# Attention and a gated unit on one core: six of nine blocks of gates and values in Strassen's seven products, with the weight sums made on chip

## The chip, the cores and the metric

The kernel runs on one core of a Trainium2 chip. The time is the device time of one execution in microseconds, from several executions on the same chip. The profile is that of one execution and names the core's engines: PE (TensorE, the matmuls; PEld is its weight load), DVE (VectorE), ACT (ScalarE), POOL (GpSimd) and SP, which here only issues DMAs. All arithmetic is on float32 data.

## The reference

`q`, `k`, `v` are (8, 8, 576, 64): eight batches of eight heads. Four heads see a local window of 32 positions, four see every 32nd position. The result, 4608 tokens by 512, goes through a gated unit with 1536 hidden columns.

```python
scores = scale * np.matmul(q, k.transpose(0, 1, 3, 2))
scores = np.where(masks[None], scores, -1000000000.0)
attn = np.exp(scores - np.max(scores, axis=-1, keepdims=True))
attn = attn / (np.sum(attn, axis=-1, keepdims=True) + 1e-09)
x = np.matmul(attn, v)                       # then reordered to (4608, 512)
gate = 1.0 / (1.0 + np.exp(-(x @ w_gate)))   # w_gate, w_val: 512 x 1536
val = x @ w_val
return (gate * val @ w_out)                  # w_out: 1536 x 512
```

## The kernel before

**Blocks and columns.** The tokens are cut into nine blocks `k` of 512 (`TB`). Blocks 0 to 7 are the first 512 positions of each batch; block 8 (`B`) gathers the 64 remaining positions of all eight (kept in `xr` by `keep_rest`, L328, until then). The hidden columns are cut into twelve groups `f` of 128 (`NF`). One (k, f) has three steps of twelve matmuls each: `glu_gate` (L385) makes the gate in PSUM bank "g" and ACT takes its sigmoid into tile `e`; `glu_val` (L393) makes the value in bank "v", DVE multiplies the two (L407); `glu_out` (L444) multiplies the result with `w_out` and adds it up over f in four banks "o0", "o1".

**Three matmuls for one product.** A factor is kept as a rounded upper part in the type float32r and the rest: `xh`, `xl` for the input, `wh`, `wl` for weights, `hh`, `hl` for the hidden block. `products` (L378) multiplies upper by upper, upper by rest and rest by upper, for each of four chunks of 128 input rows: twelve matmuls of 128 x 128 weights on 512 columns. The upper part is an ACT cast (L402), the rest a DVE subtraction (L405).

**Attention.** A pair of heads (`pair`, L163) is one step; a batch has four, each giving one chunk of 128 rows of x. A step is: load q and k (Q), scores on PE (S), mask, maximum and subtraction on DVE (F, L224 to L230), exponential on ACT (E, L234), sum, reciprocal and multiplication on DVE (N, L238 to L241), eight transposes of 32-row strips on DVE (B, L263), then the values on PE (X, L291), and from PSUM the two parts of x (H, L322, and L, L326). The pairs of batches 0 and 1 and the block 0 of the gated unit stand in an order written out by hand (`ORDER`). The 24 pairs of batches 2 to 7 are issued by `attention()` between the blocks: pair n's values and pair n + 1's scores after the gate and value of every third f of blocks 1 to 6, while `glu_out` runs one or two f behind. Scores there take banks "g" and "v", values bank "a".

**Order.** From block 1 on PE runs its instructions in the order of the program. The other engines' order is fixed by a scheduler that goes through the program in order and, where an instruction isn't ready by its own model of time, takes the next that is. Each engine then keeps that order on the chip: an instruction that waits holds all behind it. SP issues the loads and the outputs in one queue.

Of the kernel before, what the change touches and what calls it, by code (L numbers as in the profile page):

```python
# [9 lines left out]
F32 = mybir.dt.float32  # L10
# [10 lines left out]
P = 128  # L21
# [25 lines left out]
LATE = NF - 1  # L47

# [34 lines left out]
def attention_then_glu(ctx, tc, qk_l, qk_s, v_l, v_s, w_all, consts, out):  # L83
# [79 lines left out]
    def pair(b, step, space):  # L163
# [111 lines left out]
        def weigh(xp):  # L275
# [4 lines left out]
            for n in range(NBL if local else NG):  # L280
# [3 lines left out]
                for j in range(2):  # L284
# [14 lines left out]
            if local:  # L299
                full = ns // 2 * P  # L300
                src = xp.rearrange("p (r n) -> p r n", r=2)[:, :, :full].rearrange("p r (u n) -> p u r n", n=per * LB)
                main = [(src, lambda x: x[:, c, :].rearrange("p (u r n) -> p u r n", r=2, n=per * LB))]
                left = [(xp[:, full : full + REST], lambda x: x)]
            else:
# [3 lines left out]
                runs = [(0, 2 * (SS // 2), GC, 0), (BANK, full, GC, half), (BANK + full * GS, 1, STRIDE - half - full * GC, half + full * GC)]  # L308
                for at, n, r, first in runs:
                    src = xp[:, at : at + n * GS].rearrange("p (g i r) -> p i g r", i=CLS, r=GC)[:, :, :, :r]  # L310
# [16 lines left out]

        def keep_rest():  # L328
# [6 lines left out]
            L=split_low, R=keep_rest,  # L335
        )

# [3 lines left out]
    def attention():  # L341

        todo = [(b, step) for b in range(BY_PE, B) for step in range(4)]
        ahead, now = pair(*todo[0], work), None
        ahead["Q"]()
        for n, (b, step) in enumerate(todo + [(B, 0)]):
            if now:
                of, p = todo[n - 1]
                if p == 0:
                    x_tiles(of)  # L350
                    left_over(of)
                now["X"](bank("a", f"x{of}_{p}"))
                now["H"](), now["L"](), now["R"]()
            if b < B:
                now = ahead
                now["Z"]()
                if n == 0:
                    now["S"](bank("a", f"s{b}_{step}"))
                else:
                    now["S"](*(ps.tile([P, BANK], F32, tag=t, name=f"s{b}_{step}_{t}") for t in "gv"))  # L360
                now["F"](), now["V"](), now["E"](), now["N"](), now["B"]()
                if n + 1 < len(todo):
                    ahead = pair(*todo[n + 1], work)
                    ahead["Q"]()
            yield

    def split_rest():
        x_tiles(B)
        xh, xl = xs[B]
        for c in range(NC):  # L370
            for b, x in xr.items():
                cut = slice(b * REST, b * REST + x.shape[2])
                nc.scalar.copy(xh[:, c, cut], x[:, c, :])
                nc.vector.tensor_tensor(xl[:, c, cut], x[:, c, :], xh[:, c, cut].bitcast(F32), op=ALU.subtract)
# [17 lines left out]

    def glu_val(k, f, v=None):  # L393
# [3 lines left out]
        e, t = hs[k, f], work.tile([P, TB], F32, tag="t", name=f"t{k}_{f}")  # L397
        hh = work.tile([P, TB], F32R, tag="hh", name=f"hh{k}_{f}", bufs=3)
        hl = work.tile([P, TB], F32R, tag="hl", name=f"hl{k}_{f}", bufs=3)
        hs[k, f] = (hh, hl)  # L400
# [43 lines left out]
    def glu_out(k, *fs):  # L444

        if fs[0] == 0:
            two = [bank(f"o{n}", f"o{k}_{n}") for n in range(NTT // 2)]
# [73 lines left out]
    with tc.manual_schedule(engines={mybir.EngineType.PE}):  # L521
        last = [(0, NF - 1)]
        pend = attention()
        for k in range(1, NB):
            if k == B:
                split_rest()
# [97 lines left out]
```

## Time and profile before

| | us |
|---|---|
| median of 3 runs | 993.3 (992.32 to 997.05) |
| the profiled execution | 991.66 |
| its span, first to last instruction | 989.8 |

The mean granted clock of TensorE was 0.987 of full speed. A page of the profile gives each engine's busy time and its share of the span, then the chain of work that ended last, followed backwards, then groups of instructions: line, engine, operation, output and inputs, shape, count, busy time in us, mean duration in ns, and idle time of the engine before them with what ended it. Views of the trace give single instructions in order of time (start and duration in us), busy time by stretches, and waits (in total, times, longest). The whole-page rows that are used stand with the argument below.

### The profile page before, as it was taken

The page shows a single profiled execution, that of the slowest core. Times are in us where ns is not written, and L with a number is a line of the kernel's source. Part 1 is how long each engine was busy: PE and PEld are TensorE (multiplying, and loading weights), DVE is VectorE, ACT ScalarE, POOL GpSimd, SP SyncE. Part 2 cuts the span into 40 slices and gives each one's busy share as a digit, 9 for nine tenths or more (in the row PEclk, how much of TensorE's full clock was granted, in tenths as well). Part 3 has the DMA queues.
Part 4 walks back from the last instruction along what each step waited for, and adds up shares of the span by engine and source line. Part 5 has one row for each costly group of instructions (what it writes and reads, how often), then busy time and mean ns, then how long its engine had stood idle before and what let it go on. Part 6 is the DMA issues. An engine that isn't in the chain of part 4 may idle for free.

```text
span 989.8 us, 17820 instructions
## 1 busy us (share of the span) xinstructions
PE 968.3 (98%) x7840; PEld 797.7 (81%) x7840; DVE 492.4 (50%) x861; ACT 335.9 (34%) x587; POOL 3.5 (0%) x20
## 2 busy tenths in 40 slices
PE   4999999999999999999999999999999999999998
PEld 4787778888888888888888888888888888888886
DVE  6788875555555555454544555555545421112111
ACT  4787863232323233322322333223223311112111
POOL 0000000000000000000000000000000000000000
PEclk7799999999999999999999999999999999999999
DMA  7666632111211112111201121112110010001001
GB/s 262 198 185 221 220 114 68 41 53 42 95 41 53 42 63 73 53 42 51 66 28 44 42 94 42 53 42 74 62 53 17 1 44 0 1 1 43 1 1 42
DMA packets 20029, 66.00 MB, mean 67 GB/s; under 512 B 2288, under 2 KB 2672, under 8 KB 19952
## 3 DMA queue, kind: packets, MB, share of 16 engines
q1 hardware_dynamic: 18032, 58.63, 17.8%
q10 hardware_dynamic: 1920, 6.24, 2.0%
q8 instruction: 61, 1.00, 0.4%
q14 instruction: 16, 0.13, 0.0%
HBM read 55.42 MB, written 9.44 MB: 66 GB/s over the span
## 4 chain that ended last, share of the span: by engine, by line
PE 95%; DVE 2%; ACT 1%; DMA 1%; issue 0%; ACTq 0%; SPq 0%
PE o L417 29%; PE v L383 29%; PE g L383 28%; PE x L291 4%; PE s_v L208 1%; PE s_g L208 1%; DMA raw<-in_w_all 1%; PE s L208 1%; PE t L249 1%; PE gv L383 1%; ACT high L138 0%; DMA qk<-in_qk_l 0%; ACT pt L271 0%; DVE sb L241 0%; DVE mx L229 0%
## 5 line engine op out<-in xcount | busy, mean ns | idle before, releaser
L417 PE MATMUL o<-w,hh 128*128 128x512 f32 x864 | 269.6, 393 | 0.0
L383 PE MATMUL g<-xh,w 128*128 128x512 f32 x784 | 259.3, 391 | 0.0
L383 PE MATMUL v<-xh,w 128*128 128x512 f32 x784 | 259.3, 391 | 0.0
L407 DVE TENSOR_TENSOR t<-e,v 128x512 f32<-128x512 f32 x107 | 73.5, 687 | 290.6 <-PE v L383 288.3
L417 PEld LDWEIGHTS o<-w,hh 128*128 128x128 f32 x864 | 160.0, 188 | 34.2 <-ACT ob L433 0.3
L383 PEld LDWEIGHTS g<-xh,w 128*128 128x128 f32 x784 | 147.6, 188 | 31.1 <-ACT w L157 0.2
L383 PEld LDWEIGHTS v<-xh,w 128*128 128x128 f32 x784 | 147.7, 188 | 30.9
L417 PE MATMUL o<-w,hl 128*128 128x512 f32 x432 | 168.0, 389 | 0.0
L402 ACT CAST hh<-t 128x512 fp32r<-128x512 f32 x108 | 67.1, 622 | 291.5 <-DVE t L407 291.5
L383 PE MATMUL v<-xl,w 128*128 128x512 f32 x392 | 153.0, 390 | 0.0
L383 PE MATMUL g<-xl,w 128*128 128x512 f32 x392 | 153.0, 390 | 0.0
L391 ACT ACTIVATE e<-g 128x512 f32<-128x512 f32 x107 | 64.0, 598 | 155.5 <-PE g L383 154.9
L405 DVE TENSOR_TENSOR hl<-t,hh 128x512 fp32r<-128x512 f32 x108 | 74.8, 692 | 61.9 <-ACT hh L402 61.5
L263 DVE STREAM_TRANSPOSE pt<-sb 32x320 f32<-32x320 f32 (+1 forms) x192 | 103.0, 536 | 3.1
L417 PEld LDWEIGHTS o<-w,hl 128*128 128x128 f32 x432 | 81.1, 188 | 17.2
L383 PEld LDWEIGHTS v<-xl,w 128*128 128x128 f32 x392 | 73.9, 188 | 15.2
L383 PEld LDWEIGHTS g<-xl,w 128*128 128x128 f32 x392 | 73.9, 188 | 15.1
L326 DVE TENSOR_TENSOR xl<-x,xh 128x512 fp32r<-128x512 f32 (+1 forms) x64 | 24.2, 420 | 56.5 <-ACT xh L322 56.5
L291 PEld LDWEIGHTS x<-pt,vv 64*64 64x64 f32 (+1 forms) x1856 | 35.3, 142 | 13.7 <-issue 9.3
L391 ACT ACT_TABLE_LOAD x28 | 35.9, 1283 | 26.8 <-PE g L383 26.7
L238 DVE TENSOR_REDUCE mx<-sb 128x10 f32<-128x640 f32 (+1 forms) x32 | 26.3, 823 | 37.2 <-ACT sb L234 37.1
L234 ACT ACT_TABLE_LOAD x28 | 35.9, 1283 | 25.7 <-DVE sb L230 24.6
(62 smaller groups left out, 648.0 us busy)
## 6 DMA issues: line engine op xcount, KB each, us to landing
raw<-in_w_all SPq DMA_DIRECT2D x36, 512.0 KB, 3.7
qk<-in_qk_s SPq DMA_DIRECT2D x14, 599.0 KB, 5.5
vv<-in_v_l SPq DMA_DIRECT2D x13, 640.0 KB, 4.2
qk<-in_qk_l SPq DMA_DIRECT2D x14, 592.0 KB, 5.1
out<-ob SPq DMA_DIRECT2D x32, 256.0 KB, 2.0
vv<-in_v_s SPq DMA_DIRECT2D x13, 384.0 KB, 3.2
vv<-in_v_l ACTq DMA_DIRECT2D x3, 640.0 KB, 5.6
qk<-in_qk_s ACTq DMA_DIRECT2D x2, 599.0 KB, 4.5
```

The lines of the kernel that those rows point to most:

```text
L208: nc.tensor.matmul(sc[j % len(sc)][g * m : (g + 1) * m, j // len(sc) * BANK + s * kk : j // len(sc) * BANK + (s + 1) * kk], qk[d, q0 : q0 ...
L234: nc.scalar.activation(prob, prob, AF.Exp, scale=SCALE)
L238: nc.vector.tensor_reduce(row, prob, axis=AX.X, op=ALU.add)
L263: nc.vector.transpose(dst[to : to + LB, :, col : col + LB], src[rows : rows + LB, :, h * LB : (h + 1) * LB])
L291: nc.tensor.matmul(xp[j * D : (j + 1) * D, r * BANK + (u * per + g) * m : r * BANK + (u * per + g + 1) * m], v[rows, (u * per + g) * P + j ...
L326: nc.vector.tensor_tensor(dst(xs[b][1]), src, dst(xs[b][0]).bitcast(F32), op=ALU.subtract)
L383: nc.tensor.matmul(o, w, x, start=first and n == 0, stop=last and n == len(todo) - 1)
L391: nc.scalar.activation(e, g, AF.Sigmoid)
L402: nc.scalar.copy(hh, t)
L405: nc.vector.tensor_tensor(hl, t, hh.bitcast(F32), op=ALU.subtract)
L407: nc.vector.tensor_tensor(t, e, v, op=ALU.mult)
L417: nc.tensor.matmul(acc[k][i], h[:, i * P : (i + 1) * P], w, start=f == 0 and n == 0, stop=f == NF - 1 and n == 2,)
```

## The change

Blocks 3 to 8 are taken in pairs (3, 4), (5, 6), (7, 8). For a pair of blocks (rows r1, r2), two chunks of input rows at a time (c and 2 + c) and two column groups (f, f + 1), gate and value are a 2 x 2 by 2 x 2 product of submatrices. Instead of eight half products there are seven, in Winograd's form: `G1` to `G7` for the gate, `V1` to `V7` for the value. Each is 2 chunks x 3 matmuls of 512 columns.

* **Weights.** `sum_sets` makes the sums and differences of the weights of two column groups: six POOL operations, an ACT cast, a DVE subtraction and two DMAs, 24 times, two per f of block 1. `plain_sets` copies the unsummed ones. All go to a DRAM tile `sets` (3.67 MB for each of six q). The SBUF space of gate and value weights is used again afterwards: f = 0 to 6 by the x sets, 7 and 8 by hidden blocks, 9 and 10 by the ring. `load_group` streams the weights back, in the order of use, into a ring of five tiles (12 products), one transfer of SP for two products.
* **Inputs.** Values of blocks 3 to 8 are kept unsplit (`keep_raw`, K, ACT copies). `build_x` makes the seven inputs for one c: four POOL operations, seven ACT casts and seven DVE subtractions. For the first pair it stands at f = 8 and 11 of block 2, for the others in the row of `glu_out` between pairs.
* **Plans.** `superblock` runs six plans per pair. Products 1, 6, 7 and 4 follow each other in one PSUM bank (`a`), 2 and 5, 7, 3 use the other (`d`): after 1, 6 and 7 ACT copies the partial sum out and PE goes on adding in the same bank, after 2, 7 and 3 DVE adds the other bank to a copy. `A` and `B` in a plan are `glu_out` of the first block of the pair, `X` and `S` the attention's values and scores, in the gate's banks (g) or the value's (v).
* **Second block.** Its hidden blocks are kept unsplit in SBUF; after the six plans twelve `split_hidden` and `glu_out` follow, 12 matmuls each.
* **Attention earlier.** Block 2 now takes eight pairs of heads (after f = 0, 3, 6, 9 too), the plans of blocks 3 and 4 take eight, those of 5 and 6 four.
* **In `glu_val`** the product is written over `e` instead of into a tile of its own (except block 0).

```diff
+SUPER = (3, 5, 7)
+PAIRS = NF // 2
+SLOT = {p: n for n, p in enumerate("1246375")}
+RING = (("w9_0", 2), ("w9_1", 2), ("w10_0", 2), ("w10_1", 2), ("xl", 4))
+SOFAR = "G1 G2 G6 G5 G7 V1 V2 G4 G3 V6 V5 V7 A V4 V3 B"
+EARLY = "G1 Xv G2 Sv G6 G5 G7 V1 V2 G4 G3 V6 V5 V7 A Xg V4 Sg V3 B"
+MIDDLE = "G1 G2 G6 G5 G7 V1 V2 G4 G3 V6 Xg V5 Sg V7 A V4 V3 B"
+FIRST = "G1 G2 G6 Xv G5 Sv G7 V1 V2 G4 G3 V6 V5 V7 A V4 V3 B"
+END = "G1 G2 G6 G5 G7 V1 V2 G4 G3 V6 V5 V7 A Xg V4 Sg V3 B"
+PLANS = {3: [EARLY, MIDDLE, FIRST] * 2, 5: [END] * 4 + [SOFAR] * 2, 7: [SOFAR] * PAIRS}
...
+    def sum_sets(q, i, c):
+        n = (q * 2 + i) * 2 + c
+        u = spare(("t", "h0")[n % 2], f"sum{q}_{i}_{c}", F32)
+        for at, f in ((0, 2 * q), (2, 2 * q + 1)):
+            nc.gpsimd.tensor_tensor(u[:, at : at + 2], part(wh[f][i], c), part(wl[f][i], c), op=ALU.add)
+        for to, x, y, op in ((3, 2, 3, ALU.add), (2, 0, 2, ALU.subtract), (0, 3, 0, ALU.subtract), (1, 1, 0, ALU.subtract)):
+            nc.gpsimd.tensor_tensor(u[:, to], u[:, x], u[:, y], op=op)
+        h = spare("l0", f"sumh{q}_{i}_{c}", F32R)
+        nc.scalar.copy(h, u)
+        nc.vector.tensor_tensor(u.bitcast(F32R), u, h.bitcast(F32), op=ALU.subtract)
+        nc.sync.dma_start(sets[q][:, 7 * i + 3 : 7 * i + 7, 0, c], h.bitcast(F32))
+        nc.sync.dma_start(sets[q][:, 7 * i + 3 : 7 * i + 7, 1, c], u)
...
+    def build_x(k, c):
+        r1, r2 = x_raw[k], x_raw[k + 1]
+        def two_parts(p, x):
+            h, l = (t[:, c] for t in x_set[k][p])
+            nc.scalar.copy(h, x)
+            nc.vector.tensor_tensor(l, x, h.bitcast(F32), op=ALU.subtract)
...
+        two_parts("1", r1[:, c])
+        two_parts("2", r1[:, 2 + c])
+        t1 = diff(0, r2[:, c], r1[:, c])
+        t2 = diff(1, r2[:, 2 + c], t1)
+        two_parts("6", t2)
+        two_parts("5", t1)
+        two_parts("7", diff(0, r2[:, 2 + c], r2[:, c]))
+        nc.gpsimd.tensor_tensor(t2, r1[:, 2 + c], t2, op=ALU.subtract)
+        two_parts("4", t2)
+        two_parts("3", r2[:, 2 + c])
...
+                to = a if p in "1674" else d
+                w, n = ring.pop((k, q, what))
+                x = x_set[k][p]
+                for c in range(2):
+                    for j, (wi, xi) in enumerate(((0, 0), (0, 1), (1, 0))):
+                        nc.tensor.matmul(
+                            to,
+                            w[:, (wi * 2 + c) * P : (wi * 2 + c + 1) * P],
+                            x[xi][:, c],
+                            start=p in "125" and c == j == 0,
+                            stop=c == 1 and j == 2,
+                            skip_group_check=True,
+                        )
+                left[n] -= 1
+                if left[n] == 0:
+                    load_group(n + len(RING))
+                if p in "167":
...
+                    nc.scalar.copy(got[m, p], a)
+                    if p != "7":
+                        continue
+                if p == "5":
+                    continue
+                by = {"2": "1", "7": "7", "3": "6"}.get(p)
+                if by:
+                    x = got[m, by]
+                    nc.vector.tensor_tensor(x, x, d, op=ALU.add)
+                    if m == "G":
+                        nc.scalar.activation(x, x, AF.Sigmoid)
+                    else:
+                        nc.vector.tensor_tensor(x, x, got["G", by], op=ALU.mult)
...
+        for k in range(1, SUPER[0]):
             for f in range(NF):
                 glu_gate(k, f)
                 glu_val(k, f)
+                if k == 1:
+                    for _ in range(2):
+                        q, i, c = build.pop(0)
+                        if i == c == 0:
+                            plain_sets(q)
+                        sum_sets(q, i, c)
+                if k == 2 and f >= 9:
+                    for n in {9: (0, 1), 10: (2, 3), 11: (4,)}[f]:
+                        load_group(n)
                 last.append((k, f))
+                if f % 3 != 1:
+                    out_next()
                 if (k, f) == (1, 0):
+                    scores(score_banks("gv", "s1_0"))
+                elif f % 3 == 2 or (k == 2 and f % 3 == 0):
+                    values(score_banks("a", f"x{k}_{f}"))
+                    scores(score_banks("gv", f"s{k}_{f}"))
+                if f % 3 == 2:
+                    out_next()
+                if k == 2 and f == 6:
+                    set_tiles(SUPER[0])
+                if k == 2 and f in (8, 11):
+                    build_x(SUPER[0], f // 11)
+        for k in SUPER:
+            superblock(k)
...
+            for f in range(NF):
+                split_hidden(k + 1, f, hidden[f])
+                glu_out(k + 1, f)
+                if f in (0, 3):
+                    build_x(k + 2, f // 3)
```

More of the change, by code (lines that the diff above doesn't have):

```diff
@@ L334, in pair, with banks @@
             Q=load_qk, V=load_v, Z=room, S=score, F=soft, E=expo, N=norm, T=turn, B=turn_blocks, P=spread, X=weigh, H=split_high,
-            L=split_low, R=keep_rest,
+            L=split_low, R=keep_rest, K=keep_raw,
         )
+    def banks(tag, name):
+        if tag in "gv":
+            return [ps.tile([P, BANK], F32, tag=tag, name=name)]
+        two = bank(tag, name)
+        return [two[:, :BANK], two[:, BANK:]]
     def bank(tag, name):
         return ps.tile([P, 2 * BANK], F32, tag=tag, name=name)
[L341 to L374, printed above, removed]
+    x_raw = {}
+    def raw_tile(k):
+        x_raw[k] = odd.tile([P, NC, TB], F32, tag="xl" if k - 1 in SUPER else "xh", name=f"xraw{k}")
@@ new lines, in attention_then_glu, with begin_attention, scores @@
+    todo = [(b, step) for b in range(BY_PE, B) for step in range(4)]
+    line = {}
+    def begin_attention():
+        line["at"], line["ahead"] = 0, pair(*todo[0], work)
+        line["ahead"]["Q"]()
+    def scores(tiles):
+        if line["at"] == len(todo):
+            return
+        now = line["now"] = line["ahead"]
+        line["of"] = todo[line["at"]]
+        line["at"] += 1
+        now["Z"]()
+        now["S"](*tiles)
+        now["F"](), now["V"](), now["E"](), now["N"](), now["B"]()
+        if line["at"] < len(todo):
+            line["ahead"] = pair(*todo[line["at"]], work)
+            line["ahead"]["Q"]()
@@ L376, in attention_then_glu, with values, rest_raw @@
+    def values(xp):
+        now, (b, p) = line["now"], line["of"]
+        if p == 0:
+            (x_tiles if b < SUPER[0] else raw_tile)(b)
+            left_over(b)
+        now["X"](*xp)
+        if b < SUPER[0]:
+            now["H"](), now["L"](), now["R"]()
+        else:
+            now["K"](x_raw[b]), now["R"]()
+    def rest_raw():
+        raw_tile(B)
+        for b, x in xr.items():
+            nc.scalar.copy(x_raw[B][:, :, b * REST : b * REST + x.shape[2]], x)
     hs = {}
@@ L446, in glu_out @@
         if fs[0] == 0:
[L447 to L448 removed]
+            acc[k] = [x for n in ("agv" if k in (4, 5, B) else ("o0", "o1")) for x in banks(n, f"o{k}_{n}")]
         for i in (0, 2, 1, 3) if k == B else range(NTT):
@@ new lines, in split_hidden, with score_banks @@
+    def split_hidden(k, f, x):
+        hh, hl = parts_tiles(k, f)
+        nc.scalar.copy(hh, x)
+        nc.vector.tensor_tensor(hl, x, hh.bitcast(F32), op=ALU.subtract)
+    def score_banks(tags, name):
+        return [bank(tags[0], name)] if len(tags) == 1 else [ps.tile([P, BANK], F32, tag=t, name=f"{name}_{t}") for t in tags]
+    with tc.manual_schedule(engines={mybir.EngineType.PE}):
+        last.append((0, NF - 1))
+        begin_attention()
+        build = [(q, i, c) for q in range(PAIRS) for i in range(2) for c in range(2)]
+        for k in range(1, SUPER[0]):
```

158 lines of the change are left out of this document (133 added, 25 removed).

## The prediction, made before the change was timed

> **What bounds the kernel now.** I read the page's head and chain first, then busy time by stretches, then the groups of instructions, then single rows.
>
> ```profile
> span 989.8 us, 17820 instructions
> PE 968.3 (98%) x7840; PEld 797.7 (81%) x7840; DVE 492.4 (50%) x861; ACT 335.9 (34%) x587; POOL 3.5 (0%) x20
> ...
> PE 95%; DVE 2%; ACT 1%; DMA 1%; issue 0%; ACTq 0%; SPq 0%
> ...
> 0.00:60.00 60.00, 45.21 (x690) 36.82 (x691) 44.32 (x80) 36.44 (x73) 0.60 (x6) 0.80 0.68 227
> ...
> 262.00:368.00 106.00, 106.00 (x919) 87.59 (x918) 55.94 (x98) 32.66 (x54) 0.40 (x2) 1.00 0.16 54
> ...
> 790.00:895.00 105.00, 105.00 (x465) 86.92 (x464) 19.85 (x29) 17.68 (x30) 0.00 (x0) 1.00 0.04 16
> ```
>
> TensorE carries 95% of the chain that ended last. In the two later windows it is busy for the whole stretch at clock 1.00, while DVE has 56 of 106 us and ACT 33. (A window row reads: stretch, length, PE, PEld, DVE, ACT, POOL busy with counts, clock, DMA share, GB/s.) So a matmul taken out of blocks 1 to 8 is worth its whole pitch, and a wait put into TensorE's stream costs its whole length: there is no slack to catch up in. A busy row hides how long one matmul takes, because neighbours overlap; the pitch comes from the chain in order of time:
>
> ```profile
> 50.42 2.72 PE v L383 x12
> ...
> 226.17 2.94 PE o L417 x12
> ```
>
> Twelve matmuls take 2.72 us, so the pitch is 0.2267 us. The second row (0.22 us more) is the first `glu_out` behind the attention's small matmuls.
>
> **What goes.** For blocks 3 to 8, gates and values were 6 blocks x 12 f x 24 = 1728 matmuls. Now they are 3 pairs of blocks x 6 plans x 14 products x 6 matmuls = 1512. The 216 that are gone are worth 216 x 0.2267 = 49.0 us. `glu_out` and the attention keep their counts, so the floor is the run's own 991.7 us (span 989.8 plus 1.9 around it) less 49.0 = 942.7. Everything else is what TensorE newly has to wait for.
>
> **Handovers inside a plan.** A product is 6 matmuls, 1.36 us. TensorE now goes on in a bank that ACT or DVE must first have read. Four places in each plan leave one product between the two: G6 after ACT's copy of G1, G7 after that of G6, V7 after that of V6, and G5 (which overwrites the other bank) after DVE's addition of G2.
>
> ```profile
> 425.75 0.39 PE L383 MATMUL g<-xh,w 128*128 128x512 f32 x1
> ...
> 426.24 0.60 ACT L391 ACTIVATE e<-g 128x512 f32<-128x512 f32 x1 [0.95 <-PE g L383]
> ```
> ```profile
> L391 ACT ACTIVATE e<-g 128x512 f32<-128x512 f32 x107 | 64.0, 598 | 155.5 <-PE g L383 154.9
> L407 DVE TENSOR_TENSOR t<-e,v 128x512 f32<-128x512 f32 x107 | 73.5, 687 | 290.6 <-PE v L383 288.3
> L405 DVE TENSOR_TENSOR hl<-t,hh 128x512 fp32r<-128x512 f32 x108 | 74.8, 692 | 61.9 <-ACT hh L402 61.5
> L402 ACT CAST hh<-t 128x512 fp32r<-128x512 f32 x108 | 67.1, 622 | 291.5 <-DVE t L407 291.5
> ```
>
> A last matmul ends 0.16 us after the next product's start (0.39 - 0.23), ACT starts 0.10 later and a 128x512 read of PSUM takes 0.60: the bank is free 0.86 us into a product of 1.36, slack 0.50. On DVE (0.69) the slack is 0.41. By themselves these 72 places (4 x 18 plans) cost 0. They cost as soon as something sits in front on ACT or DVE. Per plan ACT gets 12 such instructions (7.2 us) and DVE 12 (8.3 us), against 108 matmuls = 24.5 us of TensorE; throughput is ample, and order is the question.
>
> **What sits in front: the softmax.** One pair of heads, with scores done by 226.17 (the row above):
>
> ```profile
> 226.12 0.69 DVE L326 TENSOR_TENSOR xl<-x,xh 128x512 fp32r<-128x512 f32 x1 [2.51 <-ACT xh L322]
> 226.73 0.49 DVE L228 TENSOR_TENSOR sb<-s_g,cst 128x324 f32<-128x324 f32 x1
> ...
> 230.16 0.83 DVE L238 TENSOR_REDUCE mx<-sb 128x12 f32<-128x648 f32 x1 [0.81 <-ACT sb L234]
> ...
> 231.50 0.83 DVE L241 TENSOR_TENSOR sb<-sb,mx 128x648 f32<-128x648 f32 x1
> 232.37 4.65 DVE L263 STREAM_TRANSPOSE pt<-sb 32x384 f32<-32x384 f32 x8
> 237.05 0.69 DVE L407 TENSOR_TENSOR t<-e,v 128x512 f32<-128x512 f32 x1
> ```
> ```profile
> 163.90 0.22 DVE L240 RECIPROCAL mx<-mx 128x10 f32<-128x10 f32 x1
> 164.03 0.63 DVE L407 TENSOR_TENSOR t<-e,v 128x512 f32<-128x512 f32 x1
> 164.57 0.82 DVE L241 TENSOR_TENSOR sb<-sb,mx 128x640 f32<-128x640 f32 x1
> ```
>
> From the end of the scores to the last transpose are 10.9 us, 10.3 without L326's subtraction, which blocks 3 to 8 no longer have there. The GLU's own DVE work slips in between dependent steps (second fence), but the eight transposes stand together, 4.65 us, and the L407 multiplication comes out behind them. Without other work they hold DVE from 6 to 10.3 us after the scores; each GLU operation that slips in moves them 0.7 later.
>
> (1) *Block 2* now takes eight pairs instead of four. At f = 0, 3, 6, 9 no `glu_out` follows the scores: the next gate needs bank g, which DVE's mask addition (0.49 us) releases 0.5 to 0.7 us later. In the next f, which has no `glu_out`, the value product ends about 6.2 us after the scores; if its multiplication misses the slot before the transposes it ends at 11.0, while the following value product wants bank v at 8.9: 2.1 us. So 0.5 to 2.8 each, four times: 2 to 11. I take 6, since 6.2 us lies right at the edge, and 1 more for `build_x` at f = 8 (7 subtractions x 0.69 on DVE). 7, bounds 2 to 13.
>
> (2) *Start of the first plan.* The last scores of block 2 are followed by one `glu_out` (2.72) and G1 (1.36), then Xv, which needs this pair's transposes: 10.3 - 4.1 = 6.2 us of waiting. The second half of `build_x` is issued at the same place; of its 4.8 us on DVE none to all comes first: 6.2 to 11.0. I take 7.5, two slipped subtractions. A wait of this length may also cost clock:
>
> ```profile
> PE t L249 <- DVE sb L241: 5.6, 1, 5.6
> ...
> 5.00:10.00 5.00, 2.95 (x128) 2.54 (x128) 2.94 (x5) 0.44 (x1) 0.00 (x0) 1.00 0.91 338
> 10.00:15.00 5.00, 0.83 (x4) 0.72 (x4) 4.69 (x9) 2.14 (x4) 0.00 (x0) 0.70 0.88 300
> 15.00:20.00 5.00, 4.17 (x156) 3.55 (x154) 4.83 (x9) 2.50 (x5) 0.00 (x0) 0.50 0.37 126
> ```
>
> TensorE's 5.6 us wait for DVE is followed by a window at 0.50. Between nothing and 5 us at half clock (2.5 us lost) I take 1. The Trainium skill, "TensorE: Matmul & The Clock Gate", Part 1, says that an idle window of about 3.4 us halves the clock until TensorE has been busy for about as long; by it the loss would be 1.7 us, an estimate from that page, and the row agrees in kind.
>
> (3) *The twelve pairs inside plans* (eight in the first pair of blocks, four in the second). Where scores stand before V3 and `glu_out` (EARLY's second, END), G2 of the next plan ends 6.8 us after them and G5 wants its bank at 8.2. If the addition slips in before the transposes the wait is 0; if not, it waits to about 11.7: 3.5. Six places, 0 to 21; the other six 0 to 1.2 each, 0 to 7. ACT adds its own block:
>
> ```profile
> L234 ACT ACT_TABLE_LOAD x28 | 35.9, 1283 | 25.7 <-DVE sb L230 24.6
> ...
> L234 ACT ACTIVATE sb<-sb 128x640 f32<-128x640 f32 (+1 forms) x32 | 23.8, 743 | 23.5 <-DVE sb L230 23.4
> ```
>
> Two table loads and an exponential are 3.3 us, and a copy right behind one load has 1.28 - 0.50 = 0.8 us to pay. Of 0 to 28 (and 0.8 x 12 = 10 from ACT) I take 7, 0.6 a pair, nearer the lower end: with three GLU operations slipped in, the transposes start after 7 us, behind G2.
>
> (4) *Weight sums in block 1*: 24 sets, each 6 POOL operations, one ACT cast (0.62), one DVE subtraction (0.69), two DMAs. From a block with the same four pairs (the window at 262) DVE rises from 56 to 73 of 106 us, ACT from 33 to 48; both hidden. No row has POOL arithmetic; the nearest are
>
> ```profile
> L188 POOL MEMSET sb<- 128x120 f32 x16 | 3.3, 205 | 739.8 <-DVE pt L263 614.9 <-PE t L253 103.7 <-PE t L249 20.9
> ```
>
> and DVE's 0.69 for 512 columns. At 0.2 to 0.9 us each (the memset's rate taken to 512 columns) the 144 operations are 29 to 130 us, against 106 us of block 1 and as much of block 2 before the data are used. The casts wait for POOL in ACT's queue with the sigmoids behind them; a gate's bank has about 4.8 us of room. 0 to 13 (0.5 a set); I take 2, because of that room. Queued behind POOL's sums are only the memsets of `room`, needed by the transposes. `build_x` of the later pairs lies under 12 `glu_out` (32.6 us), with at most 14 casts and 14 subtractions beside those of the hidden parts, 18 us on DVE: 0.
>
> (5) *Weights from DRAM*: 252 products x 256 KB = 66 MB, some 126 transfers of 512 KB on SP, each waiting for TensorE to leave a ring tile; behind a waiting one stand the attention's loads and the outputs.
>
> ```profile
> raw<-in_w_all SPq DMA_DIRECT2D x36, 512.0 KB, 3.7
> qk<-in_qk_s SPq DMA_DIRECT2D x14, 599.0 KB, 5.5
> vv<-in_v_l SPq DMA_DIRECT2D x13, 640.0 KB, 4.2
> ```
>
> A plan needs 3.67 MB in 24.5 us, 150 GB/s, with a pair's loads (1.2 MB) some 200. The first window moved 227 GB/s at a share of 0.68, that is up to 330; one transfer after another gives 142. The ring holds 12 products, 16 us, against 3.7 of landing, so several are in flight: 0. The 22 MB written in block 1 go at 208 GB/s if they are to end there, and have block 2 as reserve: 0.
>
> Sum: 942.7 + 7 + 8.5 + 7 + 2 = 967.2 on this execution. The median of the runs, 993.3, is 1.6 above it, so 968.8; I say **968**.
>
> **Rivals.** *Nearly the whole gain*: DVE's operations always slip in; only (2) and the lower ends of (1) are left, waits of 5 to 14, 948 to 957. For it: DVE and ACT are half idle. Against: eight transposes stand together in every pair that I looked at.
>
> *The softmax takes most of it*: near the upper ends of (1) to (4), 12 + 12 + 18 + 3 = 45, or 988; from 36 us of waits on, 979 to 988.
>
> *POOL and DVE hold each other up*: if each of DVE's 24 + 12 subtractions and 8 softmax steps with two SBUF operands in block 1 first waits out a POOL operation (0.2 to 0.9), DVE loses 9 to 40 us there, of which 33 are spare, though not all in the right place; TensorE sees 0 to 15, so up to 982. The Trainium skill, "SBUF — State Buffer", Who interferes with whom, says that such a DVE instruction and a POOL one that reads SBUF exclude each other. No run here shows it yet: POOL only sets memory, and does so in 20 instructions.
>
> *Slower*: the handovers are late everywhere. With 17.5 us standing from (1), (2) and (4), the 72 places decide from (49.0 - 17.5) / 72 = 0.44 us each. Two ACT instructions in front of each copy (1.2 us, less 0.50) give 0.7 x 72 = 50 us, 1010 us. For it: the order on ACT and DVE is fixed beforehand, and an exponential waiting for DVE blocks what is behind it. Against: 10 of 18 plans have a pair of heads, and the others nothing in front. If weights came one transfer at a time, 66 MB at 142 GB/s would be 465 us for plans of 441, and it would also be slower.
>
> **How the numbers follow.** Forecast (waits 14 to 36 us, 957 to 979): 0.50. Nearly whole gain: 0.15. Softmax takes most: 0.10 up to 988, and 0.09 within 0.5%, about what a measurement of this kernel can tell from no change (988.3 to 998.3). POOL against DVE: 0.05. Slower: 0.11. Faster is 0.50 + 0.15 + 0.10 + 0.05 = 0.80. The range 950 to 990 takes in the forecast, the rivals up to 988 and most of the first: 0.80.
>
> **What would show it.** The matmuls of 512 columns fall by 216 at a pitch of 0.2267. (1): in block 2, idle time of g and v ended by DVE's mask addition and multiplication. (2): one wait of 6 to 11 us at the first x of the first plan, ended by a transpose. (3): waits of up to 3.5 us at G5, ended by DVE, in plans with scores; none in the plans from block 7 on. (4): no TensorE idle in block 1. (5): no matmul that waits for a DMA. A clock below 1.00 after block 1, or matmuls waiting for the ring, would make it wrong; so would scores whose transposes no longer stand together.

## The result and the profile after

| | before | after |
|---|---|---|
| median, us | 992.8 (991.7 to 997.1, 4 runs) | 1141.6 (1141.2 to 1142.6, 4 runs) |
| the profiled execution | 991.66 | 1141.66 |
| its span | 989.8 | 1139.8 |

After divided by before is 1.149, 95% interval 1.146 to 1.153. The change costs 149 us where 25 were to be won; against the floor of 942.7 us 199 are lost instead of 24.5. Among the executions of the kernel before that stand beside the later runs, one had a granted clock of 0.677 and took 1693.1 us; it is in none of the ratios.

First the head of the page and the line of the chain by engine:

```profile
span 1139.8 us, 18423 instructions
PE 985.1 (86%) x7624; PEld 772.5 (68%) x7624; DVE 604.6 (53%) x981; ACT 429.7 (38%) x754; POOL 122.9 (11%) x188
...
PEclk9998999998898897999999999899899999999999
...
PE 46%; DVE 12%; ACT 7%; issue 1%; DMA 0%; POOL 0%; ACTq 0%; DVEq 0%
```

The count is as foreseen: 7840 - 7624 = 216 matmuls fewer. But TensorE's busy time *rises*, from 968 to 985 us, and its share of the chain falls from 95% to 46%. Two things can lengthen the busy time of fewer matmuls: a lower clock (the digits of 8 and 7 in PEclk show where), and the end of a matmul before each wait, which no neighbour overlaps any more (0.39 us against a pitch of 0.2267). The rest is idle time. The windows by stage (stretch, length, busy time of PE, PEld, DVE, ACT, POOL, clock, DMA share, GB/s) put both in place; the stretches are block 1, block 2, and the plans of each pair of blocks up to `V3` of the sixth. A block's stretch runs from the gate of its predecessor's f = 11 to that of its own:

```profile
143.71:275.35 131.64, 109.85 (x911) 87.20 (x910) 75.07 (x124) 47.27 (x81) 72.72 (x124) 0.96 0.58 180
275.35:420.30 144.95, 128.40 (x1410) 103.67 (x1408) 94.96 (x164) 56.34 (x96) 19.83 (x31) 0.91 0.33 105
437.40:645.20 207.80, 175.40 (x1608) 134.53 (x1606) 128.42 (x218) 82.16 (x141) 2.43 (x7) 0.96 0.48 153
685.36:894.10 208.74, 169.18 (x1028) 124.92 (x1026) 76.62 (x122) 58.16 (x103) 0.20 (x1) 0.94 0.38 119
933.92:1095.55 161.63, 145.87 (x619) 114.34 (x617) 47.85 (x71) 41.40 (x73) 0.00 (x0) 1.00 0.41 124
```
```profile
138.45:242.55 104.10, 104.10 (x911) 85.72 (x909) 58.42 (x103) 35.70 (x61) 0.40 (x2) 1.00 0.17 55
```

The second fence is block 1 of the kernel before: no idle time, clock 1.00. The same 911 matmuls take 27.5 us longer after the change. The clock alone, (1 - clock) x length, cost at most 5.3 + 13.0 + 8.3 + 12.5 + 0 = 39 us in these five stretches; counting only the time at half clock in which TensorE was busy, it is 31. Only the last pair, without attention beside it, runs at full clock. The waits of TensorE, grouped by what ended them (total, times, longest, us), name the rest:

```profile
PE G_o L695 <- DVE e L721: 15.6, 6, 4.6
PE g L418 <- DVE sb L239: 12.6, 5, 6.4
PE V_a L695 <- DVE h L731: 9.8, 11, 2.0
PE V_a L695 <- ACT hid L713: 9.8, 10, 2.1
PE G_o L695 <- ACT e L713: 9.1, 12, 1.2
...
PE V_a L695 <- ACT h L713: 8.2, 12, 0.7
```

Some are long and few (first line), others short and in every plan (the lines with 10 to 12 times). The short ones turn out to be the larger part, and the prediction had no price for them. In the last pair, where nothing but plans runs, one plan reads (start, duration, idle time before and what ended it):

```profile
1016.42 1.52 PE L695 MATMUL G_g<-xs,ring 128*128 128x512 f32 x6
...
1019.14 1.52 PE L695 MATMUL G_g<-xs,ring 128*128 128x512 f32 x6
...
1023.22 1.52 PE L695 MATMUL V_a<-xs,ring 128*128 128x512 f32 x6
1025.41 1.66 PE L695 MATMUL V_a<-xs,ring 128*128 128x512 f32 x6 [0.68 <-ACT h L713]
...
1032.09 3.04 PE L695 MATMUL V_a<-xs,ring 128*128 128x512 f32 x12 [0.94 <-ACT hid L713]
```
```profile
1024.77 0.58 ACT L713 COPY h<-V_a 128x512 f32<-128x512 f32 x1 [0.77 <-PE V_a L695]
```

`G1 G2 G6` (the row of `G2` lies between the first two) follow each other at the pitch of 1.36 us, just as the handover's working said: ACT reads one bank while TensorE fills the other. `V2` doesn't: it starts at 1025.41, 0.06 us after ACT's copy of `V1` ends at 1025.35. Yet `V2` writes bank `d` and the copy reads bank `a`. The difference between G and V here is how the banks were asked for: "g" and "v" are two tiles of one bank, "a" is *one* tile of two banks, cut in halves by `banks`. `V5`, in the last row, waits in the same way for the copy of `V6`. In the pair of blocks 5 and 6, whose gates and values use "o0" and "o1", also tiles of two banks, G waits like this too (`G_o L695 <- ACT e L713`, 12 times).

### The profile page after: what moved, and what is told of

It reads as the page before. It is cut to its first block, busy times and chain, and to the rows that moved or that the text cites. A ratio compares the mean times of both kernels' runs of the same rounds, so it can differ in the third digit from the quotient of the medians.

```text
span 1139.8 us, 18423 instructions
## 1 busy us (share of the span) xinstructions
PE 985.1 (86%) x7624; PEld 772.5 (68%) x7624; DVE 604.6 (53%) x981; ACT 429.7 (38%) x754; POOL 122.9 (11%) x188
## 4 chain that ended last, share of the span: by engine, by line
PE 46%; DVE 12%; ACT 7%; issue 1%; DMA 0%; POOL 0%; ACTq 0%; DVEq 0%
PE V_a L695 9%; PE o_o L455 8%; PE G_o L695 6%; PE G_g L695 5%; PE V_o L695 4%; PE o_a L455 4%; DVE pt L274 4%; PE G_v L695 3%; PE o_v L455 2%; PE o_g L455 2%; DVE e L721 1%; DVE h L731 1%; ACT e L723 1%; PE x L305 1%; ACT h L713 1%
## 5 line engine op out<-in xcount | busy, mean ns | idle before, releaser
L455 PE MATMUL o_o<-w,hh 128*128 128x512 f32 x576 | 179.2, 392 | 0.0
L695 PE MATMUL V_a<-xs,ring 128*128 128x512 f32 x504 | 133.8, 404 | 31.7 <-DVE h L731 9.8
L695 PEld LDWEIGHTS V_a<-xs,ring 128*128 128x128 f32 x504 | 91.9, 189 | 65.9 <-ACT hid L713 14.3
L455 PEld LDWEIGHTS o_o<-w,hh 128*128 128x128 f32 x576 | 107.8, 189 | 23.1
L418 PE MATMUL g<-xh,w 128*128 128x512 f32 x256 | 95.2, 433 | 27.1 <-DVE sb L239 12.6
L455 PE MATMUL o_o<-w,hl 128*128 128x512 f32 x288 | 112.3, 390 | 0.0
L695 PE MATMUL G_o<-xs,ring 128*128 128x512 f32 x252 | 74.9, 442 | 28.8 <-DVE e L721 15.6
L418 PE MATMUL v<-xh,w 128*128 128x512 f32 x256 | 88.9, 407 | 4.2 <-DVE e L445 4.1
L695 PEld LDWEIGHTS G_o<-xs,ring 128*128 128x128 f32 x252 | 51.0, 211 | 50.2 <-DVE e L721 18.2
L418 PEld LDWEIGHTS g<-xh,w 128*128 128x128 f32 x256 | 53.0, 207 | 42.5 <-DVE sb L239 13.6
L695 PE MATMUL V_o<-xs,ring 128*128 128x512 f32 x252 | 66.3, 402 | 10.8 <-ACT h L713 4.3
L695 PE MATMUL G_g<-xs,ring 128*128 128x512 f32 x288 | 74.3, 393 | 0.0
L695 PE MATMUL G_v<-xs,ring 128*128 128x512 f32 x216 | 58.7, 409 | 8.1 <-DVE e L721 8.1
L695 PEld LDWEIGHTS V_o<-xs,ring 128*128 128x128 f32 x252 | 46.1, 190 | 26.6 <-ACT h L713 6.8
L695 PEld LDWEIGHTS G_g<-xs,ring 128*128 128x128 f32 x288 | 54.0, 189 | 12.3 <-ACT e L713 0.6
L418 PEld LDWEIGHTS v<-xh,w 128*128 128x128 f32 x256 | 50.3, 197 | 16.7 <-DVE e L445 5.7
L721 DVE TENSOR_TENSOR e<-e,G_v 128x512 f32<-128x512 f32 x36 | 24.6, 684 | 61.1 <-PE G_v L695 31.9
L418 PE MATMUL g<-xl,w 128*128 128x512 f32 x128 | 54.1, 422 | 0.0
```

Of the source, the lines that this page charges most:

```text
L418: nc.tensor.matmul(o, w, x, start=first and n == 0, stop=last and n == len(todo) - 1)
L455: nc.tensor.matmul(acc[k][i], h[:, i * P : (i + 1) * P], w, start=f == 0 and n == 0, stop=f == NF - 1 and n == 2,)
L695: nc.tensor.matmul(to, w[:, (wi * 2 + c) * P : (wi * 2 + c + 1) * P], x[xi][:, c], start=p in "125" and c == j == 0, stop=c == 1 and j == ...
L721: nc.vector.tensor_tensor(x, x, d, op=ALU.add)
```

## The experiments

Theory A: several costs that stand for themselves. The waits are kept per tile, so that a tile of two banks takes away the overlap on which the handovers rest; the weight sums delay sigmoids in block 1; END puts a pair's transposes in front of `G5`; block 2 is too full. Rivals are given with each run. The base of the runs without a ratio is after's median, 1141.6 us; each is one execution. Twelve executions of the kernel before, timed beside the later ones of these runs, lie between 991.4 and 1000.3 us, so that a few us of a single execution say little, and the stage that an edit touches says more than the total. Line numbers in the rows of these runs may differ from after's by one or two.

**Single banks.** Every tile of two banks, the attention's too, becomes two tiles of one; together they still take the same eight banks.

```diff
     def banks(tag, name):
...
-        two = bank(tag, name)
-        return [two[:, :BANK], two[:, BANK:]]
+        return bank(tag, name)
...
     def bank(tag, name):
-        return ps.tile([P, 2 * BANK], F32, tag=tag, name=name)
+        return [ps.tile([P, BANK], F32, tag=f"{tag}_{n}", name=f"{name}_{n}") for n in range(2)]
```

> Every two-bank PSUM tile (a, o0, o1) becomes two tiles of one bank; nothing else changes. Theory A (a product in one bank of a two-bank tile waits for ACT's or DVE's read of the other bank, because the wait is put on the tile): the 0.68 to 0.94 us waits of V_a, V_o and G_o go, about 56 us of them plus 0.16 us of tail each, so 1067 to 1087 us, and a plan without attention takes 24.5 to 25 us in place of 27.8 (blocks 7, 8) and 31.6 (blocks 5, 6). Rival B (the handover itself is too slow, whichever bank is read): within 5 us of 1141.6.

Measured: 1061.1 us, 80.5 less, a little more than expected. From the timeline of this run, the same places in a plan of blocks 7 and 8, and the plans of these blocks up to `V4` of the sixth, in this run and in after:

```profile
928.07 2.88 PE L696 MATMUL V_a<-xs,ring 128*128 128x512 f32 x12
...
933.51 4.24 PE L696 MATMUL V_a<-xs,ring 128*128 128x512 f32 x18
```
```profile
873.89:1013.75 139.86, 139.18 (x614) 114.71 (x612) 46.15 (x69) 41.32 (x72) 0.00 (x0) 1.00 0.46 142
```
```profile
933.92:1093.25 159.33, 144.35 (x614) 113.40 (x612) 47.16 (x70) 41.38 (x72) 0.00 (x0) 1.00 0.41 126
```

The twelve matmuls of `V1 V2` run without a stop, and so do the eighteen of `V6 V5 V7`. For the same 614 matmuls the plans of blocks 7 and 8 take 139.9 us instead of 159.3, with 0.7 us idle. Of the 80.5 us 70 are in the three pairs of blocks (stage table below): 9.5, 39.9 and 20.5. The waits per tile are real and are the largest single item. What they don't explain: block 1 still takes 125.5 us, block 2 146.1.

**No weight sums.**

```diff
-        u = spare(("t", "h0")[n % 2], f"sum{q}_{i}_{c}", F32)
...
-        nc.sync.dma_start(sets[q][:, 7 * i + 3 : 7 * i + 7, 1, c], u)
+        for m, ws in ((0, wh), (1, wl)):
+            for at, f in ((3, 2 * q), (5, 2 * q + 1)):
+                nc.sync.dma_start(sets[q][:, 7 * i + at : 7 * i + at + 2, m, c], part(ws[f][i], c))
```

> The weight sums are left out: slots 3 to 6 of each set are copied from plain weights by DMA, with no POOL, ACT or DVE instruction; the traffic to DRAM and back stays. Theory A (ACT's casts and DVE's subtractions of the sums wait for POOL and hold sigmoids, masks and multiplications behind them): TensorE's waits for g and v in block 1 go, 25 us and two to three half-clock windows, so 1105 to 1117 us. Rival B (DMA traffic or the attention alone delays block 1): within 5 us of 1141.6.

This kernel leaves the sums out and copies plain weights in their place, so its result is not the product. Measured: 1129.2 us, only 12.4 less, outside the range of either theory. The windows of this run and, below them, of after:

```profile
162.65:273.36 110.71, 106.42 (x912) 86.72 (x910) 58.86 (x104) 35.67 (x61) 0.40 (x2) 0.98 0.28 89
...
60.00:170.00 110.00, 93.31 (x748) 74.05 (x747) 72.20 (x129) 67.77 (x124) 0.40 (x2) 0.89 0.95 296
```
```profile
60.00:170.00 110.00, 100.86 (x886) 81.22 (x886) 77.28 (x136) 71.81 (x130) 12.32 (x22) 0.97 0.57 177
```

Block 1 itself falls by 20.9 us to 110.7, not much less than the 25 us of waits that Theory A names. But block 0 now ends 19 us later (162.65 instead of 143.71): the copies wait for no arithmetic any more, and in a stretch of block 0 in which weights are still loaded the DMA share goes from 0.57 to 0.95, and TensorE gets through 748 matmuls instead of 886 in the same 110 us. As a measure of the sums the run is spoilt by its own side effect; its block 1 stands.

**Another place for the scores.** END's `Xg` and `Sg` go where MIDDLE has them, before `V5` and `V7`.

```diff
-PLANS = {3: [EARLY, MIDDLE, FIRST] * 2, 5: [END] * 4 + [SOFAR] * 2, 7: [SOFAR] * PAIRS}
+PLANS = {3: [EARLY, MIDDLE, FIRST] * 2, 5: [MIDDLE] * 4 + [SOFAR] * 2, 7: [SOFAR] * PAIRS}
```

> The four END plans of blocks 5 and 6 become MIDDLE: values and scores stand around V5, four products and two glu_out before the next G5. Theory A (G5 waits because DVE's addition of G2 stands behind the eight transposes): the three waits of 3.8 to 4.6 us go and with them three half-clock stretches, so 1117 to 1130 us. Rival B (the wait only moves to another product of the plan): 1136 to 1147 us.

Measured: 1124.4 us, 17.2 less, in the middle of Theory A's range. That is in part luck: blocks 5 and 6, which alone the edit touches, take 238.1 us instead of 248.6, 10.4 less, while 6.4 us are won in block 0, ahead of it. And the wait is in part moved, as Rival B has it. `G5`'s waits for DVE (`G_o L695 <- DVE e L721`) fall from 15.6 to 5.1 us, but `V3` now waits for the multiplication of `V4`, in the other half of its tile, 11.3 us instead of 2.3, 7.4 of them in one place:

```profile
PE V_o L695 <- DVE h L731: 11.3, 6, 7.4
...
PE G_o L695 <- DVE e L721: 5.1, 6, 0.9
```

What was won is mostly time at half clock, 6.8 instead of 23.9 us in these two blocks. With tiles of one bank (the next run, whose third edit concerns blocks 1 and 2) the same edit takes blocks 5 and 6 from 208.6 to 196.0 us, and the long wait doesn't come back. What END did is seen in after's timeline, TensorE and DVE around one such place:

```profile
718.67 1.66 PE L695 MATMUL G_o<-xs,ring 128*128 128x512 f32 x6 [0.73 <-ACT e L713]
724.92 0.80 PE L695 MATMUL G_o<-xs,ring 128*128 128x512 f32 x1 [4.59 <-DVE e L721]
```
```profile
719.50 4.65 DVE L274 STREAM_TRANSPOSE pt<-sb 32x384 f32<-32x384 f32 x8
724.18 0.69 DVE L721 TENSOR_TENSOR e<-e,G_o 128x512 f32<-128x512 f32 x1
```

`G5` waits 4.59 us for the addition behind the eight transposes: the bad case of step (3), 3.5 us and then some. It happens after three of the four END plans. After it the clock drops. Windows of 3.41 us around the same wait:

```profile
716.72:720.13 3.41, 2.68 (x12) 1.72 (x10) 3.26 (x7) 1.99 (x3) 0.00 (x0) 1.00 0.23 91
720.13:723.55 3.42, 0.20 (x1) 0.00 (x0) 3.35 (x6) 0.00 (x0) 0.00 (x0) 1.00 0.51 153
723.55:726.96 3.41, 2.04 (x5) 1.67 (x6) 1.27 (x3) 0.63 (x1) 0.00 (x0) 0.50 0.00 0
726.96:730.37 3.41, 2.68 (x7) 1.66 (x6) 0.00 (x0) 0.58 (x1) 0.00 (x0) 0.50 0.01 2
730.37:733.79 3.42, 3.42 (x9) 2.63 (x8) 0.00 (x0) 0.00 (x0) 0.00 (x0) 0.50 0.34 87
733.79:737.20 3.41, 2.74 (x12) 1.88 (x11) 0.69 (x1) 1.70 (x3) 0.00 (x0) 1.00 0.35 91
```

The window with 0.20 us of work is followed by *three* at half clock, 10.2 us, of which TensorE was busy for 8.1, so that they cost about 4.1. A window with 2.68 us of work (the short waits of the two-bank tiles) is harmless at full clock (first line) but doesn't end the half clock (fourth line); only the full window does. So the wait costs 4.59 + 4.1, and the small waits lengthen what the long ones begin.

**All three together.** Single banks, MIDDLE, and the whole of the weight sums on POOL.

```diff
-        nc.scalar.copy(h, u)
-        nc.vector.tensor_tensor(u.bitcast(F32R), u, h.bitcast(F32), op=ALU.subtract)
+        nc.gpsimd.tensor_copy(h, u)
+        nc.gpsimd.tensor_tensor(u.bitcast(F32R), u, h.bitcast(F32), op=ALU.subtract)
```

> Single-bank tiles, MIDDLE in blocks 5 and 6, and the cast and subtraction of the weight sums done by POOL instead of ACT and DVE, all at once. If the three causes are separate and add up: 1000 to 1040 us. If they cover for one another: above 1060. If POOL (24 sets with 2 more operations of 512 columns) now ends late and the first ring loads wait for it: a wait for DMA at the first products, and block 2's end more than 10 us later than in the single-bank run.

Measured: 1043.7 us, 97.9 less, just above the range for three causes that add up. Blocks 1 and 2 of this run, and one row of TensorE's timeline:

```profile
140.83:247.15 106.32, 104.79 (x911) 85.61 (x909) 63.90 (x106) 35.72 (x63) 80.36 (x118) 1.00 0.55 175
247.15:409.25 162.10, 127.32 (x1409) 101.81 (x1408) 96.69 (x162) 54.62 (x96) 59.28 (x86) 0.88 0.40 126
```
```profile
309.56 1.22 PE L454 MATMUL o_o<-w,hh 128*128 128x512 f32 x2 [17.21 <-DVE ob L470]
```

Block 1 is cured: 106.3 us, against 125.5 with single banks alone. What cost there was the ACT cast and the DVE subtraction waiting in the queues of the sigmoids and multiplications, not POOL's work, which has grown (80 us in block 1 instead of 73). But the sums now reach into block 2, and block 1's outputs share the tile "l0" with them: one wait of 17.21 us. Block 2 is 16.0 us longer than with single banks alone.

**Three pairs, planned anew.** Block 1's outputs get another tile, and the plans of blocks 3 and 4 are changed so that no values are due right after scores.

```diff
-PLANS = {3: [EARLY, MIDDLE, FIRST] * 2, 5: [MIDDLE] * 4 + [SOFAR] * 2, 7: [SOFAR] * PAIRS}
+DOUBLE = "G1 G2 G6 Xv G5 Sv G7 V1 V2 G4 G3 V6 V5 V7 A Xg V4 V3 Sg B"
+PLANS = {3: [MIDDLE, DOUBLE, MIDDLE, DOUBLE, MIDDLE, FIRST], 5: [MIDDLE] * 4 + [SOFAR] * 2, 7: [SOFAR] * PAIRS}
...
-        tag = ("ost", "l0", "t", "e")[i if k == B else i % 2]
+        tag = ("ost", "ost" if k == 1 else "l0", "t", "e")[i if k == B else i % 2]
```

> All three pairs of blocks, single-bank tiles, sums on POOL with block 1's outputs kept out of the sums' tile l0, MIDDLE in blocks 5 and 6, and in blocks 3 and 4 new places for the eight pairs of heads: first values after V6 of the first plan, no scores within four products and one glu_out before G5. Theory A (DVE's transposes stand before G5's addition, and the first values come too early): blocks 3 and 4 lose 25 us less than in the run with all three edits (237 us from first G to first G), the 17 us wait for l0 goes too: 1043.7 - 25 - 16 = 998 to 1010 us. Rival B (POOL, DMA or the clock set block 2 and the plans, whatever the places): above 1025.

Measured: 1018.3 us, between the two theories; still slower than before. Block 2 loses 12.8 us of its 162.1 and blocks 3 and 4 lose 12.6 of their 237.3, where 16 and 25 were expected. Stage by stage, in us, with what the matmuls alone need at full clock. (Counted: block 1 as before; block 2 is 36 x 12 matmuls, 97.9, and eight pairs of heads at (106.4 - 97.9) / 4 = 2.1; a pair of blocks is 6 x 108 and 144 matmuls, 179.5, and its pairs of heads, the last one with 4.4 from its last matmul to the end. A pair's stretch runs from its first product to that of the next pair; the 14 to 17 us between block 2's stretch and the first product are in no row.)

| stage | counted | after | single banks | planned anew |
|---|---|---|---|---|
| block 1 | 104 | 131.6 | 125.5 | 106.3 |
| block 2 | 115 | 145.0 | 146.1 | 149.3 |
| blocks 3, 4 | 197 | 248.0 | 238.5 | 224.7 |
| blocks 5, 6 | 188 | 248.6 | 208.6 | 195.2 |
| blocks 7, 8 | 184 | 205.9 | 185.4 | 185.2 |

The fewer heads a stage has, the nearer it comes to its count. What is left, some 34 us in block 2 and 28 in blocks 3 and 4, stands where eight pairs of heads were put.

**The same without the softmax of batch 3.**

```diff
-        now["Z"]()
-        now["S"](*tiles)
-        now["F"](), now["V"](), now["E"](), now["N"](), now["B"]()
+        if line["of"][0] == 3:
+            now["V"]()
+            now["tiles"]["pt"] = line["pt"]
+        else:
+            now["Z"]()
+            now["S"](*tiles)
+            now["F"](), now["V"](), now["E"](), now["N"](), now["B"]()
+            line["pt"] = now["tiles"]["pt"]
```

> As the replanned run, and scores, softmax and transposes of batch 3 (four of block 2's eight pairs) are left out; its values are taken with the last probabilities of batch 2. Theory A (block 2 loses its time to DVE's 9 us for each of the four added pairs): block 2, f = 11 to f = 11, falls from about 145 to about 112 to 118 us, 25 to 30 below the replanned run. Rival B (POOL's sums and the DMA traffic in block 2 delay it): less than 10 us below the replanned run.

Scores, softmax and transposes of batch 3 are left out, and its values are taken with the last probabilities of batch 2, so this kernel's result is not the reference's. Measured: 1004.3 us, 14 less. Block 2 of the run before and of this one:

```profile
248.11:397.37 149.26, 129.04 (x1409) 103.76 (x1408) 95.42 (x162) 54.70 (x96) 61.56 (x88) 0.90 0.43 137
```
```profile
249.66:380.49 130.83, 119.89 (x1154) 96.58 (x1152) 59.90 (x98) 41.45 (x84) 60.15 (x86) 0.95 0.44 137
```

Block 2 falls by 18.4 us, to neither theory's figure. Part of that are the missing matmuls themselves (at most the 8.5 us of four pairs of heads), so the waits and the half clock that four of the eight pairs bring are 10 to 18 of 34 us. Whether the other four bring the rest was not tried; of what is left in block 2 here, 3.46 us are one wait of the values for the load of `vv`.

**One pair of blocks only.** If the half products are worth what was counted, blocks 7 and 8 alone should win 49.0 / 3 = 16.3 us, since no attention stands beside them. `SUPER = (7,)`, single banks, sums on POOL spread over blocks 1 to 4, batch 7's heads at f = 1, 3, 5, 7 of block 6.

```diff
-SUPER = (3, 5, 7)
+SUPER = (7,)
...
-                if k == 1:
-                    for _ in range(2):
+                if k <= 4 and 4 <= f < 10:
...
+                paired = f % 3 == 2 if k < 6 else f in (1, 3, 5, 7)
```

> Only blocks 7 and 8 in seven products (72 matmuls of 512 columns less than before, 16.3 us); blocks 3 to 6 as before the change. Single-bank tiles, the weight sums wholly on POOL and spread over blocks 1 to 4, the last four pairs of heads at f = 1, 3, 5, 7 of block 6, so that no pair stands in a plan. Theory A (the products cost nothing of their own once each bank is a tile, and the loss is the preparation in blocks 1 and 2 and the attention in the plans): 992 - 16.3 + 2 to 8 us of waits = 978 to 984 us. Rival B (streaming the weights or the plans themselves cost time): 988 us or more.

Measured: 991.6 us (10 runs) against 994.1; ratio 0.996, 0.994 to 0.999. The number is Theory B's. But its cause isn't, as the windows of block 1, block 6 and the plans (up to `V4` of the sixth) show:

```profile
139.26:251.76 112.50, 106.31 (x912) 86.82 (x910) 62.38 (x106) 35.82 (x63) 39.98 (x62) 0.98 0.33 107
677.47:793.77 116.30, 111.41 (x977) 90.66 (x976) 68.52 (x109) 44.14 (x80) 12.17 (x10) 1.00 0.19 60
801.93:944.32 142.39, 141.78 (x626) 117.10 (x624) 46.75 (x70) 41.95 (x73) 0.00 (x0) 1.00 0.47 146
```

The plans have no fault: 142.4 us with 0.6 idle. 8.4 us are lost in block 1, whose first scores the change had moved to the gates' banks, and about 6 in block 6 (against 110.3 in the next run), where the value products wait four times (0.87, 1.17, 1.80 and 1.06 us) for DVE's multiplication.

**The same with two places put in order.** Block 1's first scores go to "a" as before the change; block 6 has one `glu_out` behind every f instead of two behind odd ones.

```diff
-                    scores(score_banks("gv", "s1_0"))
+                    scores(score_banks("a", "s1_0"))
...
-                if f % 3 != 1 if k < 6 else f > 7 or f % 2:
+                if f % 3 != 1 if k < 6 else f > 7:
                     out_next()
...
-                if paired:
+                if paired or (k == 6 and f < 7):
                     out_next()
```

> The kernel of e6 with two edits of order: block 1's first scores go to the two banks of "a" again, as in the kernel before (in e6 they share g and v with the gates: waits of 2.65, 0.38 and 3.16 us in block 1 and 3.4 us at half clock), and block 6 puts one output product behind every block of 128 features instead of two at odd ones and none at even ones (in e6 the values waited 0.87, 1.17, 1.80 and 1.06 us for DVE's multiply there). Theory A (what e6 lacks to its expectation of 978 to 984 us are these places and nothing else, so that the half products themselves bring what was counted): block 1 falls from 112.5 us to 104 to 106.5, block 6 by 3 to 6 us, and the time to 976 to 984 us. Theory B (the waits only move, since the softmax that fills ACT and DVE is the same): blocks 1 and 6 together fall by less than 4 us, and the time stays at 987.5 us or above.

Measured: **978.0 us** (974.9 to 981.7, 6 runs) against 992.9; ratio 0.985, 0.982 to 0.988. Theory A holds. The stretches of block 1, blocks 2 to 5, block 6 and the plans, again up to `V4` of the sixth:

```profile
141.42:246.40 104.98, 104.49 (x912) 85.57 (x910) 61.94 (x106) 35.72 (x63) 40.84 (x62) 1.00 0.36 115
246.40:672.10 425.70, 425.70 (x3681) 351.87 (x3680) 226.75 (x400) 131.80 (x224) 95.12 (x140) 1.00 0.28 91
672.10:782.38 110.28, 110.28 (x978) 91.00 (x976) 68.51 (x109) 43.72 (x80) 12.16 (x10) 1.00 0.20 64
790.54:932.79 142.25, 141.77 (x625) 117.03 (x624) 46.74 (x70) 41.95 (x73) 0.00 (x0) 1.00 0.46 146
```

TensorE is idle for 0.5 us in these 641 us before the plans, with POOL making sums beside it in blocks 1 to 4. Of the 16.3 us counted 14.9 arrive. This is the fastest of the kernels here.

## Why the prediction was wrong, step by step

* **The gain** (216 matmuls x 0.2267 = 49.0) was right: the count falls by 216, and one third of it, taken alone, brings 14.9 of 16.3 us.
* **"By themselves these 72 places cost 0"** is the step that failed. Its working, ACT free 0.50 us before the bank is wanted, holds where gate and value have a tile each (`G_g`, `G_v`). It assumed that a wait is kept for each bank. For `V_a`, `G_o` and `V_o` it is kept for the tile of two banks, so that a product also waits for the read of the *other* half: in the undisturbed plan above 0.68 us before `V2`, 0.94 before `V5` and, 0.78 us, before `V3`. These are not the four places that were weighed, and in blocks 5 and 6 there are about six such waits a plan. 80.5 us with what follows, shown by single banks. The rival "slower" had handovers that are late everywhere, but with a wrong mechanism, instructions queued in front on ACT and DVE; its 50 us and 1010 us were too small.
* **(1) block 2**: 7 expected, bounds 2 to 13, measured 30. The waits named are there (in block 2, `g` ended by the mask addition, five times, 9.4 us in all; `v` ended by the multiplication, 2.1 us), with others that weren't: the attention's values wait seven times, 5.0 us in all, for transposes. Together 16.6 us of waits, a little over the upper bound, and 11 to 13 of clock on top, which had no term. What makes the transposes late is settled for half of it at most (above).
* **(2) first plan**: right in the wait, too small in the clock, and together near the 8.5 us taken.

```profile
445.48 0.43 PE L305 MATMUL x<-pt,vv 64*64 64x32 f32 x4 [6.56 <-issue]
```

  6.6 us, against 7.5 taken. The profile names nothing that ended it; the pair's transposes start at 444.37. For the clock 1 us was allowed. From 443.70 on it is at half for 10.24 us, and behind the wait TensorE is busy for 6.6 of them, a loss of 3.3; in the single banks run, where the wait is also 6.6, it is at half for 13.65 us, a loss of 3.8. The kernel before already had a longer stretch than the 5 us taken as the worst case: from 12.0 us on, within and behind its wait of 5.6 us, it was at half clock for 17.07 us.
* **(3) plans with heads**: 7 was taken out of 0 to 28, the guess that the addition mostly slips in before the transposes. It came out behind them after three of the four END plans (4.59, 3.81 and 4.64 us) and after the second EARLY (4.88 us), 17.9 us in all without the clock. In the first EARLY the transposes of the other pair held up `G3` (2.57 us), a place that was not counted. END alone costs 10.4 us in its blocks with tiles of two banks, and 12.7 with tiles of one.
* **(4) sums in block 1**: 2 taken, bounds 0 to 13. Block 1 lost 27.5 us, of which 19 to 21 go with the sums (20.9 without them; 19.2 with cast and subtraction on POOL, on single banks). The mechanism was named (casts wait for POOL with sigmoids behind them), its size was not, and one part was missed. From the waits in block 1 of after:

```profile
ACT sumh L583 <- POOL sum L581: 36.5, 10, 4.6
ACT sumh L583 <- DMA sets<-sumh: 13.2, 7, 3.0
```

  ACT stands still for POOL ten times, up to 4.6 us, and seven times for the DMA that writes the cast before it to DRAM, since all casts use one tile "l0"; this wait had no term. Per set 20.9 / 24 = 0.9 us, not 0.5 at most. With the cast and the subtraction on POOL, and single banks, block 1 loses 2.2 us in all. What the other 6 to 8 us are was not separated; block 1's first scores, which the change moved to the gates' banks, are one candidate (in the run with one pair of blocks 8.4 us were lost with them there, 0.9 without).
* **(5) weights from DRAM**: 0 taken, right; no matmul of a plan waits for a DMA in any of these runs.
* **The clock** was the item without a proper term: one wait, 1 us. It takes 31 to 39 us in the five stretches, inside the figures of (1) to (4) and of the tiles, and a clock below 1.00 after block 1 was one of the prediction's own signs of being wrong. It was not taken away by itself in any run.
* **POOL against DVE** (the rival with 982) is real but small. From the groups by form of after, DVE subtractions of one shape, those of the hidden parts and those of `build_x` whose input POOL makes:

```profile
L738 DVE TENSOR_TENSOR hl<-h,hh 128x512 fp32r<-128x512 f32 x36 | 24.9, 692 | 24.5 <-ACT hh L737 24.4
...
L627 DVE TENSOR_TENSOR xs<-xd,xs 128x512 fp32r<-128x512 f32 x24 | 27.4, 1150 | 2.9 <-ACT xs L626 2.1
```

  692 ns become 1150 on average. Eight of the 24 overlap no POOL operation and take 683 ns on average, the 16 that do overlap one take 1384. The Trainium skill, "SBUF — State Buffer", Who interferes with whom, has the two engines exclude each other on shared ports; the trace agrees in kind. In block 1, cured with POOL busy for 80 of 106 us, it shows in no wait of TensorE's.

Single banks (80.5), MIDDLE on top of them in blocks 5 and 6 (12.7) and the sums' cast and subtraction on POOL in block 1 (19.2) come to 112.4 of the 149 + 25 us between forecast and result. The run with all three gained 97.9, for its block 2 was 16.0 us longer. The rest lies mostly in block 2 and in blocks 3 and 4, where the heads' softmax is shown to be at work but not measured to its end.

## What to carry to other kernels

Before an overlap between two PSUM banks is counted on, look whether the two are one tile for whatever keeps the waits; where they are, ask for them separately. Work that is moved to spare time on slower engines has to stay there as a whole: half a step handed back to a busy engine's queue blocks what stands behind it. A change worth a few per cent in matmuls is best brought in first where nothing else runs beside it, and every stage compared with its count.

## What the runs showed of the hardware

The granted clock follows a grid of 3.41 us. In after and in the single banks run I laid the idle time of TensorE in each window from block 1 on against the clock of the next. From full clock, all windows with more than 2.1 us idle were followed by half clock; of those with up to 1.1 us idle, none was, and in between it went both ways. From half clock, all windows with up to 0.4 us idle were followed by full clock, all with more than 0.75 by another half one. So a gap of 0.73 us is free in one state and may keep the clock down in the other. The Trainium skill, "TensorE: Matmul & The Clock Gate", Part 1, tells of a free-running window of 4096 cycles and about 3.4 us; the trace agrees with the grid, and shows in addition that windows that are partly idle hold the half clock, so that a 4.59 us wait brought 10.2 us of it.

POOL's arithmetic, of which no row existed before, measured in block 1 of after:

```profile
L581 POOL TENSOR_TENSOR sum<-sum 128x128 f32<-128x128 f32 x80 | 39.3, 504 | 3.1
L579 POOL TENSOR_TENSOR sum<-w 128x256 f32<-128x256 f32 x41 | 33.2, 830 | 61.8 <-DMA sets<-sum 34.7 <-DVE w L172 20.6 <-DVE sb L252 6.0
```

504 ns for 128 columns and 830 for 256, inside the bounds of 0.2 to 0.9 us; not the work, but who waited for it, was the cost.
